# A fused retention and two-layer MLP kernel: the low part of the first eight weight tiles by a GpSimd subtraction instead of an adding DMA

## The chip, the cores and the metric

One NeuronCore of a Trainium2 chip runs the whole program. The metric is device time in microseconds (us), the median of several executions. Engines are named as in the profile: PE (TensorE), PEld (its weight loads), DVE (VectorE), ACT (ScalarE), POOL (GpSimd), SP (SyncE, which only issues DMAs here).

## What is computed

A retention layer (2 batches, 8 heads, 768 positions, head size 64) gives 1536 rows of 512 numbers; two MLPs follow, each 512 to 2048 to 512.

```python
for t in range(S):                                   # retention, y is [B, H, S, D]
    state = gamma * state + outer(k[:, :, t], v[:, :, t])
    y[:, :, t] = scale * einsum('bhd,bhde->bhe', q[:, :, t], state)
x = y.transpose(0, 2, 1, 3).reshape(1536, 512)
h = x @ w1_in;  x = softplus(h) @ w1_out             # maximum(h,0) + log1p(exp(-|h|))
h = x @ w2_in;  out = (h * clip(h + 3, 0, 6) / 6) @ w2_out
```

The four weight matrices come as 8-byte floats; the kernel gets them as pairs of 32-bit words.

## The kernel before

**Precision.** PE multiplies in a format with fewer mantissa bits than float32 (F32R). So every operand of the MLPs is kept as two tiles: a high part (the value rounded to F32R) and a low part (value minus high part). A product takes three matmuls: high by high, high by low, low by high.

**Weights.** The four matrices make 64 weight tiles of 128 x 512. `fetch` (L73) loads one as 512 KB of raw words on SP's queue. `convert` (L83) turns it into float32 in `w` and then into `w_parts`, high part in `t[:, 0]`, low part in `t[:, 1]`: ACT scales `raw`; DVE clamps it, shifts it, and merges it with two operations on two SBUF tiles each (L90 to L93, two TENSOR_SCALAR and two SCALAR_TENSOR_TENSOR in the profile); ACT writes minus the rounded value into `t[:, 1]` (L95); a DMA on POOL's queue adds `w` to it in place (L96); ACT writes the rounded value into `t[:, 0]` (L97). A buffer of `w` is free again when its adding DMA has landed.

**Order.** The list at L104 to L107 fixes which tile is converted when: four tiles of the first matrix (EARLY = 4), then tiles of the second and the first in turn, so that tiles number 4 and 6 (counted from 0) belong to the second matrix; then the second MLP's 32 tiles. `done[1]` counts converted tiles.

**Loops.** Four units of 128 rows of the retention run alone (L296). Then eight more units run in turn with the first eight of 96 steps (L144); after that the steps run alone. A step multiplies one 128-wide slice of the hidden layer for 512 rows (`gemm1`, 12 matmuls of 128 x 512, needs one tile of the first matrix), runs the activation over ACT and DVE, splits the result into `hi` (ACT) and `lo` (POOL for the first 16 steps, DVE later), and multiplies the slice of two steps before into the output banks (`gemm2`, 12 matmuls, needs one tile of the second matrix). The first 16 steps need tiles 0 to 31, two a step. A retention unit puts its score mask `pt`, its output `on` and the state update `bd` on DVE, and the decayed `vs`, the low part `x_lo` and the fading of `bd` on POOL.

A scheduler orders each engine's instructions after the first section (`nc.on = False` at L303) by its own estimate of times, so an edit in one place can move instructions elsewhere. A helper records nearly every instruction under L31, so tiles are told apart by name, not by line.

Of the kernel before, what the change touches and what calls it, by code (L numbers as in the profile page):

```python
# [10 lines left out]
F32 = mybir.dt.float32  # L11
F32R = mybir.dt.float32r
U32 = mybir.dt.uint32
AF = mybir.ActivationFunctionType
ALU = mybir.AluOpType
# [25 lines left out]
@with_exitstack  # L41
def kernel(ctx, tc, q, k, v, w1_in, w1_out, w2_in, w2_out, tq, tk, tc_, tg, out):
    nc = InOrder(tc)
    B, H, S, D = q.shape
    NT, DM = out.shape
    DFF = w1_in.shape[1]
    NP = H // 2
    KD = DM // P
    NF = DFF // P
    C = P  # L50
    NCH = S // C
    CH = 512
    chunks1 = [(0, 0, 512), (1, 0, 512), (2, 0, 512)]
    chunks2 = [(0, 0, 512), (1, 0, 512), (2, 0, 512)]
    LAG = 2
    EARLY = 4

    tc.nc.scalar.preload_act_table_set("softplus")

    xpool = ctx.enter_context(tc.tile_pool(name="xpool", bufs=1))  # L60
    x_hi = [xpool.tile([P, KD, CH], F32R, name=f"x_hi{c}") for c in range(NT // CH)]
    x_lo = [xpool.tile([P, KD, CH], F32R, name=f"x_lo{c}") for c in range(NT // CH)]

    win_p = ctx.enter_context(tc.tile_pool(name="win", bufs=NF))
    wout_p = ctx.enter_context(tc.tile_pool(name="wout", bufs=NF))
    psum = ctx.enter_context(tc.tile_pool(name="psum", bufs=1, space=PSUM))
    raw_p = ctx.enter_context(tc.tile_pool(name="raw", bufs=3))
    cv_p = ctx.enter_context(tc.tile_pool(name="cv", bufs=2))

    w_in_t, w_out_t, raws = {}, {}, {}  # L70
    words = {0: (w1_in.bitcast(U32), w1_out.bitcast(U32)), 1: (w2_in.bitcast(U32), w2_out.bitcast(U32))}

    def fetch(m, o, f):  # L73
        raw = raw_p.tile([P, CH, 2], U32, tag="raw", name="raw")
        src = words[m][o]
        if o:
            nc.sync.dma_start(out=raw.rearrange("p n t -> p (n t)"), in_=src[f * P:(f + 1) * P, :])
        else:
            nc.sync.dma_start(out=raw.rearrange("p (k n) t -> p k (n t)", k=KD),
                              in_=src[:, 2 * f * P:2 * (f + 1) * P].rearrange("(k p) f -> p k f", p=P))  # L80
        raws[m, o, f] = raw

    def convert(m, o, f):  # L83

        raw = raws.pop((m, o, f))
        low, y = raw[:, :, 0], raw[:, :, 1]

        w = cv_p.tile([P, CH], U32, tag="w", name="w")
        nc.scalar.activation(y.bitcast(F32), y.bitcast(F32), AF.Copy, scale=2.0 ** -112)
        nc.vector.tensor_scalar(y.bitcast(F32), y.bitcast(F32), -TOP, TOP, ALU.max, ALU.min)  # L90
        nc.vector.tensor_scalar(w, y, 3, None, ALU.logical_shift_left)
        nc.vector.scalar_tensor_tensor(w, y, 0x80000000, w, ALU.bitwise_and, ALU.bitwise_or)
        nc.vector.scalar_tensor_tensor(w, low, 29, w, ALU.logical_shift_right, ALU.bitwise_or)  # L93
        t = (wout_p if o else win_p).tile([P, 2, CH], F32R, tag="w", name="w_parts")
        nc.scalar.activation(t[:, 1], w.bitcast(F32), AF.Copy, scale=-1.0)  # L95
        nc.gpsimd.dma_start(out=t[:, 1].bitcast(F32), in_=w.bitcast(F32), accum_op=ALU.add)  # L96
        nc.scalar.activation(t[:, 0], w.bitcast(F32), AF.Copy)  # L97
        if o:
            w_out_t[m, f] = t
        else:  # L100
            w_in_t[m, f] = t.rearrange("p a (k n) -> p a k n", k=KD)

    NU = B * NCH
    order = [(0, 0, f) for f in range(EARLY)]  # L104
    for f in range(NF):
        order += [(0, 1, f)] + [(0, 0, f + EARLY)] * (f + EARLY < NF)
    order += [(1, 0, f) for f in range(NF)] + [(1, 1, f) for f in range(NF)]  # L107
    done = [0, 0]

    def fetch_weights(n):  # L110
        while done[0] < min(len(order), n):
            fetch(*order[done[0]])
            done[0] += 1

    def feed(n):

        n = min(n, len(order))
        while done[1] < n:
            fetch_weights(done[1] + (1 if nc.on else 2))
            convert(*order[done[1]])  # L120
            done[1] += 1

    banks = psum.tile([P, 8, CH], F32, name="banks")
    free = list(range(8))

    def bank(hold=False):

        i = free.pop(0)
        if not hold:
            free.append(i)  # L130
            return banks[:, i, :]
        return i, banks[:, i, :]

    def release(i):
        free.append(i)

    def first(f):
        return EARLY + 2 * (f + 1) - max(0, f + 1 + EARLY - NF)

    step, last, n_steps = moe(ctx, tc, nc, out, x_hi, x_lo, w_in_t, w_out_t, chunks1, chunks2, NF, KD, DM, CH, LAG, feed, first, bank, release)  # L140
    s = 0
    with ExitStack() as actx:
        unit = attention(actx, tc, nc, q, k, v, tq, tk, tc_, tg, x_hi, x_lo, CH, bank, feed, fetch_weights)
        for u in range(CH // P, NU):  # L144
            unit(u)
            step(s)
            s += 1
    while s < n_steps:
        step(s)
        s += 1  # L150
# [298 lines left out]
```

## Time and profile before

| what | value |
|---|---|
| median of 3 runs | 633.73 us (632.96 to 635.1) |
| the profiled execution | 632.11 us, its span 630.3 us |
| PE busy over the span | 600.6 us (95%) |
| DVE busy | 352.4 us (56%) |
| ACT busy | 281.1 us (45%) |
| POOL busy | 116.5 us (18%) |
| adding DMAs `w_parts<-w` | 64, 256 KB each |

The span is what the trace covers; 1.8 us lie around it. Shares are means over stages that are limited by different engines: the retention alone (to about 29 us), the stage in which weights are converted for the first 16 steps (about 29 to 187 us), and the rest, in which PE runs without gaps. Matmul ends are modelled, so a busy PE is not PE at its peak.

### The profile page before, as it was taken

The numbers are of one execution on the slowest core, as the hardware profiler recorded it, in microseconds if no ns is written. First come the engines' busy times: TensorE is split into PE (matmuls) and PEld (weight loads), VectorE is DVE, ScalarE is ACT, GpSimd is POOL, SyncE is SP. The second block draws the span as 40 slices with busy tenths as digits, with TensorE's granted clock in tenths as the row PEclk, the third lists the DMA queues.
The fourth block names the chain that finished last, engine by engine and source line by source line (L and its number), as shares of the span: only waits on it lengthen the run. The fifth ranks groups of instructions, "written<-read, shape, count | busy, mean of one in ns | idle before, by whom it ended". The sixth has DMA issues, their size and how long they took to land.

```text
span 630.3 us, 7793 instructions
## 1 busy us (share of the span) xinstructions
PE 600.6 (95%) x2963; PEld 493.1 (78%) x2963; DVE 352.4 (56%) x567; ACT 281.1 (45%) x481; POOL 116.5 (18%) x126
## 2 busy tenths in 40 slices
PE   7957979799989999999999999999999999999997
PEld 6846767678768888888887878888888888888886
DVE  4569988898856333357576789932232222422223
ACT  3327556667655333356556677832222222222221
POOL 1735655444420000011111122300000000000000
PEclk9979979799999999999999999999999999999999
DMA  9988986798750000025558688810010000100001
GB/s 193 227 230 222 255 212 152 185 214 203 168 131 1 0 1 0 1 43 125 113 138 216 151 203 218 198 33 1 0 68 0 1 0 2 68 0 1 0 1 67
DMA packets 70662, 63.70 MB, mean 101 GB/s; under 512 B 40160, under 2 KB 56800, under 8 KB 70624
## 3 DMA queue, kind: packets, MB, share of 16 engines
q1 hardware_dynamic: 61408, 46.42, 25.5%
q0 software_dynamic: 9216, 16.78, 16.1%
q8 instruction: 23, 0.38, 0.3%
q14 instruction: 15, 0.12, 0.1%
HBM read 43.26 MB, written 3.15 MB: 74 GB/s over the span
## 4 chain that ended last, share of the span: by engine, by line
PE 60%; DVE 10%; issue 6%; DMA 4%; ACT 4%; POOL 1%; DVEq 0%; POOLq 0%; ACTq 0%
PE banks L31 60%; DVE w L31 5%; DMA raw<-in_moe_w_in_dram 3%; DVE raw L31 2%; ACT w_parts L31 1%; DVE g L31 1%; ACT e L31 1%; DMA w_parts<-w 1%; DVE e L31 1%; ACT raw L31 1%; ACT hi L31 1%; POOL lo L31 1%; DVE lo L31 1%; DVE pt L31 0%; POOL w_parts L31 0%
## 5 line engine op out<-in xcount | busy, mean ns | idle before, releaser
L31 PE MATMUL banks<-x_hi,w_parts 128*128 128x512 f32 x768 | 255.2, 393 | 5.5 <-DMA w_parts<-w 5.5
L31 PEld LDWEIGHTS banks<-x_hi,w_parts 128*128 128x128 f32 x768 | 145.0, 189 | 36.4 <-DMA w_parts<-w 5.7
L31 PE MATMUL banks<-x_lo,w_parts 128*128 128x512 f32 x384 | 150.2, 391 | 0.0
L31 PE MATMUL banks<-hi,w_parts 128*128 128x512 f32 x384 | 127.0, 392 | 0.7 <-ACT hi L31 0.4
L31 PE MATMUL banks<-w_parts,hi 128*128 128x512 f32 (+1 forms) x386 | 118.5, 388 | 0.5 <-DVE g L31 0.5
L31 DVE SCALAR_TENSOR_TENSOR w<-raw,w 128x512 uint32<-128x512 uint32 x128 | 102.6, 801 | 2.0
L31 DVE SCALAR_TENSOR_TENSOR g<-e,banks 128x512 f32<-128x512 f32 x48 | 33.0, 688 | 125.2 <-ACT e L31 125.2
L31 POOL DMA_DIRECT2D w_parts<-w x64 | 55.9, 874 | 238.8 <-ACT w_parts L31 181.8
L31 ACT ACTIVATE w_parts<-w 128x512 fp32r<-128x512 f32 x128 | 74.3, 624 | 39.4 <-DVE w L31 38.7
L31 ACT ACTIVATE e<-banks,three 128x512 f32<-128x512 f32 x48 | 32.9, 686 | 127.6 <-PE banks L31 127.6
L31 ACT ACTIVATE hi<-g 128x512 fp32r<-128x512 f32 x96 | 60.6, 631 | 59.9 <-DVE g L31 59.1
L31 PEld LDWEIGHTS banks<-hi,w_parts 128*128 128x128 f32 x384 | 71.9, 188 | 17.1 <-ACT hi L31 1.6
L31 PEld LDWEIGHTS banks<-w_parts,hi 128*128 128x128 f32 x386 | 72.3, 188 | 15.8 <-DVE g L31 0.9
L31 PEld LDWEIGHTS banks<-x_lo,w_parts 128*128 128x128 f32 x384 | 72.7, 189 | 15.0 <-issue 0.3
L31 DVE TENSOR_TENSOR lo<-g,hi 128x512 fp32r<-128x512 f32 x80 | 55.3, 691 | 47.2 <-ACT hi L31 47.2
L31 PE MATMUL banks<-lo,w_parts 128*128 128x512 f32 x192 | 75.5, 393 | 2.3 <-POOL lo L31 2.1
L31 PE MATMUL banks<-w_parts,lo 128*128 128x512 f32 (+1 forms) x193 | 74.9, 388 | 0.0
L31 DVE SCALAR_TENSOR_TENSOR e<-g,banks 128x512 f32<-128x512 f32 x48 | 32.8, 683 | 33.0 <-ACT g L31 32.8
L31 ACT ACTIVATE raw<-raw 128x512 f32<-128x512 f32 x64 | 42.6, 668 | 17.0 <-DMA raw<-in_moe_w_in_dram 17.0
L31 DVE TENSOR_TENSOR g<-g,e 128x512 f32<-128x512 f32 x48 | 33.2, 691 | 27.4 <-ACT e L31 27.3
L31 PEld LDWEIGHTS banks<-lo,w_parts 128*128 128x128 f32 x192 | 36.0, 188 | 11.7 <-POOL lo L31 3.6
L31 ACT ACTIVATE g<-banks 128x512 f32<-128x512 f32 x48 | 28.3, 589 | 37.1 <-PE banks L31 36.7
(45 smaller groups left out, 413.8 us busy)
## 6 DMA issues: line engine op xcount, KB each, us to landing
raw<-in_moe_w_in_dram SPq DMA_DIRECT2D x32, 512.0 KB, 4.2
w_parts<-w POOLq DMA_DIRECT2D x64, 256.0 KB, 4.8
raw<-in_moe_w_out_dram SPq DMA_DIRECT2D x32, 512.0 KB, 4.5
q<-in_q_dram SPq DMA_DIRECT2D x12, 256.0 KB, 5.6
v<-in_v_dram SPq DMA_DIRECT2D x12, 256.0 KB, 4.9
k<-in_k_dram SPq DMA_DIRECT2D x11, 256.0 KB, 5.2
out_dram<-ob SPq DMA_DIRECT2D x11, 256.0 KB, 2.0
k<-in_k_dram SPq DMA_DIRECT2D x2, 128.0 KB, 2.7
```

The source lines that it names most:

```text
L31: ins = getattr(self.engine, op)(*args, **kwargs)
```

## The change

For the tiles converted while `done[1] < 8`, ACT writes the high part first, and POOL subtracts it from `w` into `t[:, 1]`; the negated copy and the adding DMA are gone for these eight tiles. The other 56 tiles are made as before.

```diff
         t = (wout_p if o else win_p).tile([P, 2, CH], F32R, tag="w", name="w_parts")
-        nc.scalar.activation(t[:, 1], w.bitcast(F32), AF.Copy, scale=-1.0)
-        nc.gpsimd.dma_start(out=t[:, 1].bitcast(F32), in_=w.bitcast(F32), accum_op=ALU.add)
-        nc.scalar.activation(t[:, 0], w.bitcast(F32), AF.Copy)
+        if done[1] < 2 * EARLY:
+            nc.scalar.activation(t[:, 0], w.bitcast(F32), AF.Copy)
+            nc.gpsimd.tensor_tensor(t[:, 1], w.bitcast(F32), t[:, 0].bitcast(F32), ALU.subtract)
+        else:
+            nc.scalar.activation(t[:, 1], w.bitcast(F32), AF.Copy, scale=-1.0)
+            nc.gpsimd.dma_start(out=t[:, 1].bitcast(F32), in_=w.bitcast(F32), accum_op=ALU.add)
+            nc.scalar.activation(t[:, 0], w.bitcast(F32), AF.Copy)
```

The scheduler's order moves with it. On PE, just after the last state update of the section that runs alone (`vs,k`), stood in the kernel before, with what each row waits for (DMASW is an adding DMA's semaphore):

```order
L31 MATMUL banks<-vs,k 128x128 x4
L31 MATMUL banks<-qT,kT 128x128 [waits Activation_49]
L31 MATMUL banks<-x_hi_59,w_parts 128x512 [waits Activation_49]
L31 MATMUL banks<-x_lo_62,w_parts 128x512 [waits Pool_49]
L31 MATMUL banks<-qT,kT 128x128 x7
L31 MATMUL banks<-x_hi_59,w_parts 128x512 [waits DMASW0_49]
L31 MATMUL banks<-x_hi_59,w_parts 128x512
```

In the changed kernel the same place reads:

```order
L31 MATMUL banks<-vs,k 128x128 x4
L31 MATMUL banks<-x_hi_59,w_parts 128x512 [waits Activation_49]
L31 MATMUL banks<-x_lo_62,w_parts 128x512 [waits Pool_49]
L31 MATMUL banks<-x_hi_59,w_parts 128x512 [waits Pool_49]
L31 MATMUL banks<-x_hi_59,w_parts 128x512
L31 MATMUL banks<-x_lo_62,w_parts 128x512
```

The first matmul that needs the low part of tile 0 waits for POOL and no longer for a DMA, and the scores `qT,kT` of the next unit stand behind the whole first `gemm1`.

On POOL, from the fade of `bd` in the fifth unit on, stood before:

```order
L31 TENSOR_TENSOR bd_112<-bd_112,tc_sb 64x4x64 [waits DVE_49,Pool_49]
L31 DMA w_parts<-w 128x512 [waits Activation_49]
L31 TENSOR_TENSOR vs<-v,tk_sb 128x512 [waits DMAHW3_49,Pool_49]
L31 TENSOR_TENSOR x_lo_63<-on,x_hi_60 128x4x128 [waits Activation_49]
L31 DMA w_parts<-w 128x512 [waits Activation_49] x2
L31 TENSOR_TENSOR lo<-g,hi 128x512 [waits Activation_49]
L31 TENSOR_TENSOR x_lo_63<-on,x_hi_60 128x4x128 [waits Activation_49]
```

In the changed kernel:

```order
L31 TENSOR_TENSOR bd_112<-bd_112,tc_sb 64x4x64 [waits DVE_49,Pool_49]
L31 TENSOR_TENSOR w_parts<-w,w_parts 128x512 [waits Activation_49,Pool_49]
L31 TENSOR_TENSOR x_lo_63<-on,x_hi_60 128x4x128 [waits Activation_49]
L31 TENSOR_TENSOR vs<-v,tk_sb 128x512 [waits DMAHW3_49]
L31 TENSOR_TENSOR w_parts<-w,w_parts 128x512 [waits Activation_49]
L31 TENSOR_TENSOR vs<-v,tk_sb 128x512 [waits DMAHW6_49]
L31 TENSOR_TENSOR lo<-g,hi 128x512 [waits Activation_49]
L31 TENSOR_TENSOR w_parts<-w,w_parts 128x512 [waits Activation_49]
L31 TENSOR_TENSOR x_lo_63<-on,x_hi_60 128x4x128 [waits Activation_49]
```

Each subtraction is one more reader and writer of SBUF among those that POOL had.

On DVE, around the shift into `w` of tile 11 (the shifts are the rows `w<-raw`), stood before, with the wait for the adding DMA of tile 8 (number 0 of its semaphores for the second time):

```order
L31 SCALAR_TENSOR_TENSOR w<-raw,w 128x512 [waits DVE_49]
L31 TENSOR_SCALAR raw<-raw 128x512 [waits DMAHW7_49,Activation_49]
L31 TENSOR_SCALAR w<-raw 128x512 [waits DMASW0_49,DVE_49]
L31 SCALAR_TENSOR_TENSOR w<-raw,w 128x512 [waits DVE_49]
L31 TENSOR_TENSOR on<-banks,tq_sb 128x512 [waits PE_49,Pool_49]
```

In the changed kernel tile 11's shift has no such wait, and the one for the DMA of tile 8 (there the first of all) comes at tile 12:

```order
L31 TENSOR_SCALAR raw<-raw 128x512 [waits DMAHW6_49,Activation_49]
L31 TENSOR_SCALAR w<-raw 128x512 [waits DVE_49]
L31 SCALAR_TENSOR_TENSOR w<-raw,w 128x512 [waits DVE_49]
L31 TENSOR_SCALAR raw<-raw 128x512 [waits DMAHW0_49,Activation_49]
L31 TENSOR_TENSOR on<-banks,tq_sb 128x512 [waits PE_49,Pool_49]
L31 TENSOR_SCALAR w<-raw 128x512 [waits DMASW0_49,DVE_49]
```

The ring of `w` buffers is one deeper by these waits.

## Rows read from the trace of the kernel before

**Rows 1.** The page's busy times by engine, and its chain that ended last.

```profile
PE 600.6 (95%) x2963; PEld 493.1 (78%) x2963; DVE 352.4 (56%) x567; ACT 281.1 (45%) x481; POOL 116.5 (18%) x126
PE 60%; DVE 10%; issue 6%; DMA 4%; ACT 4%; POOL 1%; DVEq 0%; POOLq 0%; ACTq 0%
```

**Rows 2.** Busy time by stretch: length, engines (instructions), granted PE clock, DMA share, GB/s.

```profile
40.00:60.00 20.00, 13.85 (x90) 11.35 (x91) 14.29 (x20) 10.68 (x20) 6.17 (x6) 0.84 0.94 245
60.00:80.00 20.00, 19.72 (x129) 14.73 (x130) 19.71 (x29) 11.37 (x21) 13.95 (x12) 1.00 1.00 240
120.00:160.00 40.00, 40.00 (x199) 32.63 (x199) 36.37 (x60) 27.00 (x48) 18.35 (x17) 0.98 0.81 194
29.04:192.00 162.96, 140.98 (x800) 112.24 (x799) 134.96 (x209) 96.31 (x173) 76.12 (x74) 0.94 0.80 193
```

**Rows 3.** The chain around 186 us: start, length, what.

```profile
185.31 1.28 POOL lo L31
186.63 108.92 PE banks L31 x479
```

**Rows 4.** Timeline of tile 0 (start, length, engine, operation, [idle before]), and its DMA's landing.

```profile
33.63 1.15 ACT L31 ACTIVATE w_parts<-w 128x512 fp32r<-128x512 f32 x2 [2.68 <-DVE w L31]
34.60 1.02 POOL L31 DMA_DIRECT2D w_parts<-w  x1 [1.73 <-ACT w_parts L31]
42.90 1.22 PE L31 MATMUL banks<-x_hi,w_parts 128*128 128x512 f32 x2 [5.51 <-DMA w_parts<-w]
DMA to landing us min/median/max: 8.3/8.3/8.3
```

**Rows 5.** Timeline of DVE where it stood idle for adding DMAs or their followers.

```profile
43.36 0.43 DVE L31 TENSOR_SCALAR w<-raw 128x512 uint32<-128x512 uint32 x1 [1.95 <-DMA w_parts<-w]
43.82 0.69 DVE L31 SCALAR_TENSOR_TENSOR w<-raw,w 128x512 uint32<-128x512 uint32 x1
47.79 0.69 DVE L31 SCALAR_TENSOR_TENSOR e<-g,banks 128x512 f32<-128x512 f32 x1 [3.28 <-ACT g L31]
48.86 0.43 DVE L31 TENSOR_SCALAR raw<-raw 128x512 f32<-128x512 f32 x1 [0.38 <-ACT raw L31]
88.16 0.43 DVE L31 TENSOR_SCALAR w<-raw 128x512 uint32<-128x512 uint32 x1 [1.26 <-DMA w_parts<-w]
180.41 0.43 DVE L31 TENSOR_SCALAR w<-raw 128x512 uint32<-128x512 uint32 x1 [2.68 <-DMA w_parts<-w]
```

**Rows 6.** Timeline of PE: its last gap of the conversion stage.

```profile
186.63 0.50 PE L31 MATMUL banks<-lo,w_parts 128*128 128x512 f32 x1 [0.85 <-POOL lo L31]
```

**Rows 7.** Groups over the whole span: busy us, mean ns of one, idle before.

```profile
L31 DVE SCALAR_TENSOR_TENSOR w<-raw,w 128x512 uint32<-128x512 uint32 x128 | 102.6, 801 | 2.0
L31 DVE TENSOR_SCALAR raw<-raw 128x512 f32<-128x512 f32 x64 | 32.5, 510 | 5.5 <-ACT raw L31 5.2
L31 DVE TENSOR_SCALAR w<-raw 128x512 uint32<-128x512 uint32 x64 | 32.0, 500 | 11.4 <-DMA w_parts<-w 11.1
L31 POOL DMA_DIRECT2D w_parts<-w x64 | 55.9, 874 | 238.8 <-ACT w_parts L31 181.8 <-DVE w L31 56.8
L31 POOL TENSOR_TENSOR lo<-g,hi 128x512 fp32r<-128x512 f32 x16 | 22.3, 1395 | 26.6 <-ACT hi L31 26.6
```

**Rows 8.** Timeline of DVE and POOL where their work met, or did not.

```profile
51.46 5.07 DVE L31 SCALAR_TENSOR_TENSOR w<-raw,w 128x512 uint32<-128x512 uint32 x2
51.56 1.46 POOL L31 TENSOR_TENSOR lo<-g,hi 128x512 fp32r<-128x512 f32 x1
54.05 1.20 POOL L31 TENSOR_TENSOR vs<-v,tk_sb 128x512 f32<-128x512 f32 x1
84.42 1.47 POOL L31 TENSOR_TENSOR lo<-g,hi 128x512 fp32r<-128x512 f32 x1
84.68 1.28 DVE L31 TENSOR_TENSOR pt<-banks,tm_sb 128x512 f32<-128x512 f32 x2
```

**Rows 9.** Timeline of PE after a long wait for `pt`, and after a short one.

```profile
85.42 2.07 PE L31 MATMUL banks<-qT,bd 128*128 128x128 f32 x8 [3.18 <-DVE pt L31]
99.85 1.16 PE L31 MATMUL banks<-qT,bd 128*128 128x128 f32 x8 [1.27 <-DVE pt L31]
```

## The prediction

> **What bounds the kernel now.** I read the busy times and the chain that ended last first [rows 1]. PE is busy for 95% of the span, but a share of 10% of the chain lies on DVE, so some stage is not PE's. The chain in order of time says which: the last thing before an unbroken run on PE is a POOL subtraction that ends at 186.6 us, and from 186.63 us on 479 matmuls follow each other [rows 3]. All that comes later is PE's own and this change doesn't touch it. So the time moves by what the conversion stage, 29 to 187 us, moves.
>
> The table by stretch shows who is full there. DVE was busy 134.96 of 162.96 us between 29 and 192 us, 19.71 of 20 us from 60 to 80 us and 36.37 of 40 us from 120 to 160 us; PE was full too in those two stretches, but had 13.85 of 20 us from 40 to 60 us [rows 2]. ACT, with 96.31 of 162.96 us, and POOL, with 76.12, had room. The reader should see that DVE and PE take turns at being late, and that DVE, which has to convert 32 tiles in this stage, sets the pace for most of it: PE's last gap, at 186.63 us, is for a `lo` whose input came late from DVE [rows 6].
>
> **What the change removes.** Tile 0 shows the old price. ACT had its two copies done from 33.63 us on, POOL took 1.02 us to issue the adding DMA at 34.60 us, and the data landed 8.3 us after the issue; PE stood 5.51 us until 42.90 us [rows 4]. POOL's subtraction of the same shape and types exists already: `lo<-g,hi` takes 1.395 us on average [rows 7]. POOL ended its former work before ACT's copy did (it stood 1.73 us ahead of the DMA [rows 4]), so the low part of tile 0 should be there at about 33.6 + 0.6 (half of ACT's 1.15 for two) + 1.4 = 35.6 us instead of 42.9. PE's order has the whole first `gemm1` at that place, so its wait all but goes.
>
> PE's 5.5 us are not the gain, because DVE, not PE, is late after 49 us. What counts is the time that DVE stood still because of this DMA: 1.95 us for a buffer of `w` and 3.28 us for the first activation, which PE made late [rows 5]. **Term one: minus 5.2 us.** The 0.38 us behind it [rows 5] I leave out: ACT's order there moves too.
>
> The second place is the ring of `w` buffers. Tile 11 waited 1.26 us for the adding DMA of tile 8, and a late tile waited 2.68 us [rows 5]. With the ring one deeper by the order's waits, I count the first in full. The second only matters as far as PE waited behind it, 0.85 us [rows 6]. **Term two: minus 2.1 us.** It lies between 0, if the scheduler's new order has DVE wait elsewhere, and 3.9, the two waits together.
>
> ACT loses no copy that matters: it has one copy less in each of eight tiles, 0.6 us each, on an engine with room, so I cost that at nothing; its cover is ACT's idle time, 163 less 96 us. The 8 DMA issues that leave POOL give 8 x 0.874 = 7.0 us back [rows 7], the subtractions take 8 x 1.395 = 11.2. That 4.2 us more lies in POOL's idle time, 163 less 76 us, and costs nothing by itself. Behind a subtraction on POOL stand `vs`, `x_lo` and `lo`; each is late by at most the difference of 0.5 us a tile, which PE's backlog of matmuls covers from 60 us on [rows 2].
>
> **What the change adds: POOL beside DVE.** DVE's operations on SBUF tiles stand still while POOL works on SBUF. At 51.46 us two merges, 0.69 us each when undisturbed [rows 5], took 5.07 us, and ended 1.3 us after the last of three POOL operations between 51.56 and 55.25 us [rows 8]. That is 3.7 us lost to 3.7 us of POOL. But at 84.42 us a POOL subtraction ran its 1.47 us, while DVE, which read PSUM for `pt`, kept its 1.28 us for two [rows 8]: nothing lost. So the price of a subtraction is between 0 and its own length.
>
> The mean comes from the groups. Merges averaged 801 ns against 690 undisturbed, over 128 of them 14.2 us; the clamps 510 against 430, over 64, 5.1 us; the shifts 500 against 430, 4.5 us: 23.8 us in all [rows 5, 7]. POOL's work other than DMA issues in the stage was 76.12 less 32 x 0.874 = 48.2 us [rows 2, 7]. So DVE lost 0.49 us for each us of POOL. Eight subtractions of 1.395 us are 11.2 us, and **term three is plus 5.5 us**, between 0 and 11.2. I take the mean, since the eight are spread over the same mixture of DVE's work. The order bears this out in part: behind tile 1's shift stand `e` and both `pt`, which read PSUM, but tiles 2, 3 and 6 meet merges and shifts.
>
> On this the Trainium skill, SBUF — State Buffer, section Who interferes with whom, says that the two engines share one port pair as an exclusive lock, and that an instruction with two SBUF inputs, or in a two-port mode, waits for the whole of the other's instruction. The merges at 51.46 us agree. Taken alone the rule would make term three 11.2 us; the sum above doesn't use it.
>
> **Sum.** -5.2 - 2.1 + 5.5 = -1.8 us. Against the profiled execution that is 632.1 - 1.8 = 630.3 us; its time stands 1.6 us under the median of the runs, and the forecast is for a median, so 633.7 - 1.8 = **631.9 us**. A measurement of this kernel can tell about 0.3%, 1.9 us, from no change, so this lies on the border.
>
> **Rival 1: the locks fall on covered work.** If the eight subtractions meet DVE mostly while it reads PSUM, as at 84.42 us, term three is 0 and the gain is 7.3 us: 626.4 us. For it speaks tile 1's place. Against it speaks the mean, and that DVE's conversions are the larger part of its work here.
>
> **Rival 2: each subtraction locks DVE for its whole length.** The place is DVE between 34 and 75 us, where the eight subtractions are. Then term three is 11.2 us, and the sum +3.9 us: 637.6 us, slower. It decides from 7.3 / 8 = 0.91 us of lost DVE time a subtraction, 65% of its length. For it speaks 51.46 us, where POOL operations back to back kept DVE out entirely, and that the new order sets subtractions next to `x_lo`, `vs` and `lo`. A late `pt` would add to it: after 3.18 us of waiting for `pt`, PE's next eight small matmuls took 2.07 us, at the half of its two clock levels, against 1.16 after a wait of 1.27 us [rows 9]. The page named above is the rule behind this rival. Against it speaks that the mean loss is 49%.
>
> **Rival 3: the early tiles buy nothing.** PE is ahead at 40 us, and DVE waits as long elsewhere, for `pt`'s inputs or for raw tiles, because the conversion order is the same. Then the first two terms and the third cancel, 633.7 us. For it speaks that DVE's work is unchanged in number; against it that the two waits of 1.95 and 3.28 us have no other cause than the DMA.
>
> **How the numbers follow.** Forecast 0.40, with term three between 35% and 65% of 11.2 us, so 630.3 to 633.7 us; half of that is faster by over 0.3%. Rival 1 has 0.23, rival 2 0.24, rival 3 0.13. Faster: 0.20 + 0.23 = 0.43. Within 0.3%: 0.18 from the forecast and 0.11 from rival 3, 0.29. Slower: 0.24 of rival 2 and 0.04 of what the scheduler's new order may cost in the other two, 0.28. The range reaches from rival 1 to rival 2: 626.0 to 637.7 us. The forecast's own range is 630.3 to 633.7 us.
>
> **What would show it.** In the changed profile, PE's wait of 5.5 us at 42.9 us should be gone and the first `gemm1` be over by about 39 us. DVE's two idle pieces of 1.95 and 3.28 us should be gone. Merges, clamps and shifts should take some 5.5 us more in all than 102.6 + 32.5 + 32.0 us: near 0 proves rival 1, near 11 rival 2. The unbroken run on PE should begin near 185 us instead of 186.6, and be as long as before. I am wrong if PE has new gaps after 60 us for `pt` or tiles, with its clock at the half level behind them, or if the stage after 187 us changes.

## The result and the profile after

The changed kernel took 624.85 us in the median (623.2 to 626.26, 4 runs), the kernel before 633.35 us beside it (631.57 to 635.1, 4 runs). The ratio is 0.9874, with a 95% interval of 0.984 to 0.9908: 1.26% or 8.0 us faster. (Here and below the ratio compares runs taken side by side and is not exactly the quotient of the two medians, which would be 0.9866.) The forecast was 631.9 us with a range of 626.0 to 637.7, so the time fell 1.15 us below the range. The profiled execution of the changed kernel is 623.2 us, its span 621.4 us, 8.9 us less than the 630.3 of before.

The page's busy times by engine, and its chain that ended last, answer to [rows 1]:

```profile
PE 597.2 (96%) x2963; PEld 491.9 (79%) x2963; DVE 355.6 (57%) x567; ACT 277.9 (45%) x473; POOL 122.3 (20%) x126
PE 67%; DVE 9%; issue 4%; ACT 3%; POOL 1%; DMA 1%; DVEq 0%; ACTq 0%; POOLq 0%
```

The busy time by stretch answers to [rows 2] (length, engines with instructions, granted PE clock, DMA share, GB/s):

```profile
40.00:60.00 20.00, 17.66 (x117) 13.91 (x114) 19.91 (x27) 10.48 (x20) 11.84 (x9) 0.86 0.84 218
60.00:80.00 20.00, 16.32 (x105) 12.63 (x104) 19.77 (x27) 10.57 (x19) 13.22 (x11) 0.89 0.75 189
120.00:160.00 40.00, 39.58 (x190) 32.32 (x187) 36.09 (x60) 29.28 (x52) 19.08 (x18) 1.00 0.83 198
29.04:192.00 162.96, 145.41 (x834) 117.31 (x833) 144.60 (x218) 98.90 (x175) 82.81 (x74) 0.96 0.74 180
```

DVE now is full from 40 to 80 us, 19.91 and 19.77 of 20 us, where it had 14.29 from 40 to 60 us [rows 2]. The timeline of tile 0 answers to [rows 4]; of POOL, and of PE:

```profile
33.96 1.28 POOL L31 TENSOR_TENSOR w_parts<-w,w_parts 128x512 fp32r<-128x512 f32 x1 [0.33 <-ACT w_parts L31]
```

```profile
35.26 0.77 PE L31 MATMUL banks<-x_hi,w_parts 128*128 128x512 f32 x1
...
38.76 0.39 PE L31 MATMUL banks<-x_hi,w_parts 128*128 128x512 f32 x1
```

The first `gemm1` runs from 35.26 to 39.1 us without a gap. The end of the stage, on DVE (the late wait of [rows 5]) and on PE [rows 6]:

```profile
171.50 0.43 DVE L31 TENSOR_SCALAR w<-raw 128x512 uint32<-128x512 uint32 x1 [2.43 <-DMA w_parts<-w]
```

```profile
177.72 0.50 PE L31 MATMUL banks<-lo,w_parts 128*128 128x512 f32 x1 [0.79 <-POOL lo L31]
```

PE's last gap ends at 177.72 us where it ended at 186.63. That is 8.9 us, all of the difference between the spans, so all of the gain arose in the conversion stage. The groups over the span answer to [rows 7] (busy us, mean ns, idle before):

```profile
L31 DVE SCALAR_TENSOR_TENSOR w<-raw,w 128x512 uint32<-128x512 uint32 x128 | 102.0, 797 | 1.9
L31 DVE TENSOR_SCALAR raw<-raw 128x512 f32<-128x512 f32 x64 | 35.1, 548 | 5.5 <-ACT raw L31 5.3
L31 DVE TENSOR_TENSOR g<-g,e 128x512 f32<-128x512 f32 x48 | 34.4, 716 | 27.2 <-ACT e L31 27.2
L31 DVE TENSOR_SCALAR w<-raw 128x512 uint32<-128x512 uint32 x64 | 32.7, 511 | 8.1 <-DMA w_parts<-w 7.7
```

Merges, clamps and shifts took 169.8 us after 167.1, and `g<-g,e`, which reads two SBUF tiles as well, 34.4 after 33.2. Its row in the kernel before:

```profile
L31 DVE TENSOR_TENSOR g<-g,e 128x512 f32<-128x512 f32 x48 | 33.2, 691 | 27.4 <-ACT e L31 27.3
```

In all, DVE lost 3.9 us more, where 5.5 was forecast. With that the sum would be -5.2 - 2.1 + 3.9 = -3.4 us, and -8.0 was measured. What made up the rest is what the experiments are for.

### The profile page after: what moved, and what is told of

Read it like the earlier page. It is cut to its first block, busy times and chain, and to the rows that moved or that the text cites. A ratio compares the mean times of both kernels' runs of the same rounds, so it can differ in the third digit from the quotient of the medians.

```text
span 621.4 us, 7753 instructions
## 1 busy us (share of the span) xinstructions
PE 597.2 (96%) x2963; PEld 491.9 (79%) x2963; DVE 355.6 (57%) x567; ACT 277.9 (45%) x473; POOL 122.3 (20%) x126
## 4 chain that ended last, share of the span: by engine, by line
PE 67%; DVE 9%; issue 4%; ACT 3%; POOL 1%; DMA 1%; DVEq 0%; ACTq 0%; POOLq 0%
PE banks L31 67%; DVE w L31 5%; DVE raw L31 1%; ACT w_parts L31 1%; DVE g L31 1%; DMA raw<-in_moe_w_in_dram 1%; ACT e L31 1%; DVE e L31 1%; DVE lo L31 1%; ACT hi L31 1%; POOL lo L31 0%; POOL bd L31 0%; DVE pt L31 0%; POOL w_parts L31 0%; DVE bd L31 0%
## 5 line engine op out<-in xcount | busy, mean ns | idle before, releaser
L31 DVE SCALAR_TENSOR_TENSOR w<-raw,w 128x512 uint32<-128x512 uint32 x128 | 102.0, 797 | 1.9
L31 POOL DMA_DIRECT2D w_parts<-w x56 | 49.0, 876 | 220.4 <-ACT w_parts L31 163.5
L31 ACT ACTIVATE w_parts<-w 128x512 fp32r<-128x512 f32 x120 | 69.9, 624 | 42.3 <-DVE w L31 37.7
L31 DVE TENSOR_TENSOR g<-g,e 128x512 f32<-128x512 f32 x48 | 34.4, 716 | 27.2 <-ACT e L31 27.2
```

Source lines behind the costliest of these rows:

```text
L31: ins = getattr(self.engine, op)(*args, **kwargs)
```

## Experiments: parts of the change, and its two prices

Ratios below are to the kernel before, measured beside each run, with 95% intervals; 0.01 is 6.3 us.

**Tile 0 alone, and tiles 1 to 7 alone.**

```diff
-        if done[1] < 2 * EARLY:
+        if done[1] < 1:
```

> Only tile 0 gets its low part by the GpSimd subtraction, tiles 1 to 63 by the adding DMA. Start-up theory (the 8.3 us landing of tile 0's DMA is nearly the whole cost, and the lead is kept because TensorE and VectorE then stop waiting for each other): 6 to 9 us faster than before, 625 to 627.5 us. Theory that every early tile's landing counts: one eighth to a third of the gain, 1 to 3 us, 630.5 to 632.5 us. Theory that the scheduler's new order is what helps: any time between 624 and 634 us, with no tie to the wait of 5.5 us.

Measured: 626.99 us, ratio 0.9896 (0.9854 to 0.9939), -6.6 us.

```diff
-        if done[1] < 2 * EARLY:
+        if 1 <= done[1] < 8:
```

> Tile 0 by the adding DMA as before, tiles 1 to 7 by the GpSimd subtraction. Start-up theory: the 5.5 us wait of TensorE is still there, so at most 2 us faster than before, 631.5 to 634 us. Theory that every early tile counts: 5 to 8 us faster, 625.5 to 628.5 us. Scheduler theory: anything between 624 and 636 us.

Measured: 630.13 us, ratio 0.9952 (0.9933 to 0.9972), -3.0 us. Tile 0 has the larger part of the gain, as term one had it. Each of the two runs has an order of its own, though, so this is not the work alone. The order of the run with tile 0 alone differs from that of the kernel before in one short stretch only, between 34 and 57 us: some 20 of PE's 2963 matmuls, 30 of DVE's 567 rows and 14 of ACT's and POOL's, and two loads just ahead of it. One subtraction and this stretch make 6.6 us.

**The gain without the lock, and the lock without the gain.** In the first run ScalarE makes the low part as a scaled copy, so that neither a DMA nor POOL is needed (the values differ); in the second POOL's eight subtractions are added to the kernel before.

```diff
-            nc.gpsimd.tensor_tensor(t[:, 1], w.bitcast(F32), t[:, 0].bitcast(F32), ALU.subtract)
+            nc.scalar.activation(t[:, 1], w.bitcast(F32), AF.Copy, scale=2.0 ** -13)
```

> For the first eight tiles the low part is written by one ScalarE copy (a scaled copy of w, so the low part is not the remainder), with neither the GpSimd subtraction nor the adding DMA: the cover without VectorE's lock. If the eight subtractions cost what the two traces say (VectorE busy 3.2 us more between the same two points): 3 us faster than the changed kernel, 621 to 623 us. If they cost nothing on the way to the end: as the changed kernel, 624 to 626 us. If they cost their length (11.2 us): 614 us.

Measured: 619.14 us, ratio 0.9776 (0.974 to 0.9812), -14.2 us.

```diff
         nc.scalar.activation(t[:, 0], w.bitcast(F32), AF.Copy)
+        if done[1] < 2 * EARLY:
+            nc.gpsimd.tensor_tensor(spare, w.bitcast(F32), t[:, 0].bitcast(F32), ALU.subtract)
```

> The kernel before, with one more GpSimd subtraction of the same shape into a spare tile for each of the first eight tiles, nothing removed: the lock without the cover. Mean lock price of the record (0.49 us of VectorE a us of GpSimd): plus 5.5 us, 638 to 640 us. Price by the two traces: plus 3 us, 636 to 637 us. Whole-length lock: plus 11, 644 us. Covered work: within 1 us of before.

Measured: 639.85 us, ratio 1.0109 (1.0077 to 1.0141), +6.9 us. Read together these said: the lock costs some 6 to 7 us, a little over term three, and its removal uncovers 14 us where terms one and two had 7.3. So the gain looked twice too small.

**Where the 14 us are: buffers held, traffic, or issue.** To the run with ScalarE's copy an adding DMA into a spare tile was added, which nobody waits for: reading `w` (its buffer is held until it lands), reading `w_parts` (it is not held), and reading 4 columns of `w` only. In all three POOL also zeroes the spare tiles, from 1.6 to 5.4 us, ahead of the other work.

```diff
+            nc.gpsimd.dma_start(out=SPARE[done[1]], in_=w.bitcast(F32), accum_op=ALU.add)
```

> As e3 (low part of the first eight tiles by a ScalarE copy, not the remainder), plus for each of the eight an adding DMA of the same size from w into a spare tile that nobody reads: traffic, issue and the hold on the w buffer are back, only TensorE's wait for the landing is gone. If the 14 us that e3 gained lie in TensorE's waits for landings: still 12 to 14 us under before, 618 to 621 us. If they lie in the w ring that the landings hold: back to within 4 us of before, 629 to 633 us.

Measured: 623.13 us, ratio 0.9868 (0.9834 to 0.9902).

```diff
+            nc.gpsimd.dma_start(out=SPARE[done[1]], in_=t[:, 1].bitcast(F32), accum_op=ALU.add)
```

> As e5, but the spare adding DMA reads the finished low part and not w, so the w buffers come free early: only the traffic and the issue are back. If the traffic of eight adding DMAs is what costs: close to before, 629 to 633 us. If not: as e3, 618 to 621 us. The difference to e5 is the price of the hold on w.

Measured: 623.82 us, ratio 0.9873 (0.9849 to 0.9896). The two are the same, so holding the buffers costs nothing that can be seen, though here ScalarE's later copies waited 7.1 us for these DMAs. (The orders of the two differ, in some 160 of DVE's rows.) Both lose some 6 us against the run without DMAs, which I first put down to the traffic of 8 x 256 KB. The third run tests this:

```diff
+            nc.gpsimd.dma_start(out=SPARE[done[1]][:, :4], in_=w[:, :4].bitcast(F32), accum_op=ALU.add)
```

> As the run in which ScalarE makes the low part of the first eight tiles by a scaled copy (so these low parts hold other values, and no subtraction runs), and in which an adding DMA of the tile was kept; here that kept DMA takes only 4 of the 512 columns: POOL still issues eight DMAs (0.87 us each in the trace of before), but 2 KB in place of 256 KB moves. If the eight DMAs cost their 6 us by what they move (ScalarE alone 619.1 us against 623.1 with the DMAs), this run gives about 619 us, with raw tiles landing in some 4 to 5 us as without them. If the cost is in their issue on POOL, or in the other order that the scheduler makes around eight more DMAs, it stays at about 623 us.

Measured: 624.31 us, ratio 0.9888 (0.9862 to 0.9915). With 2 KB in place of 256 KB a DMA the loss stays, 7.1 us against the run without DMAs. This run has nearly the order of the first of the three (PE's and ACT's rows are the same, nine of DVE's stand elsewhere), so the two differ by what the DMAs move and by little else. The theory of the traffic falls; left are the issue on POOL, and the order that the scheduler makes around eight more instructions.

**How many tiles.** The same change for four and for sixteen tiles:

```diff
-        if done[1] < 2 * EARLY:
+        if done[1] < 4:
```

> The change for the first four tiles alone. Tile 0 alone gave -6.6 us, the eight -8.2. If each further tile saves some traffic (0.75 us a tile) and pays a lock (0.8 us a tile), the curve is flat and this gives about 626 us, -7. If tiles 4 to 7 are the ones that gain nothing and only lock DVE, it is better than the eight: 622 to 623 us. If the gain comes from the ring of buffers of w, whose wait at tile 11 only the whole eight removes, it stays near tile 0 alone, 627 us.

Measured: 619.31 us, ratio 0.9813 (0.9786 to 0.984), -11.8 us: faster than both kernels.

```diff
-        if done[1] < 2 * EARLY:
+        if done[1] < 16:
```

> The change for the first sixteen tiles. If traffic saved and lock paid cancel for each further tile, about 624 us, as with eight. If locks cost more where DVE is full (60 to 130 us), eight more of them at 0.8 us a tile without cover give some 630 us. If the transfers are still what the later tiles wait for, another 3 us less, 621 us.

Measured: 631.57 us, ratio 1.0001 (0.9981 to 1.002): nothing gained. From one tile to four, eight and sixteen the gain goes 6.6, 11.8, 8.0, 0.0 us. A fixed price and a fixed gain for each tile would not give this curve.

**DVE in place of POOL.**

```diff
-            nc.gpsimd.tensor_tensor(t[:, 1], w.bitcast(F32), t[:, 0].bitcast(F32), ALU.subtract)
+            nc.vector.tensor_tensor(t[:, 1], w.bitcast(F32), t[:, 0].bitcast(F32), ALU.subtract)
```

> The low part of the first eight tiles by a subtraction on DVE instead of POOL: the adding DMAs are gone as in the change, and what is paid is DVE's own time, eight times about 0.7 us (a merge of the same shape takes 0.69 us undisturbed), with no lock. If the end moves by DVE's time one for one, the run with ScalarE (619.1 us) plus 5.6 gives 624.7 us, the same as the change. If the lock costs more than DVE's own work would (0.8 us a tile from the runs, and 1.39 us of POOL each), this is faster than the change, 622 to 624 us. If the order on DVE with eight more instructions is what counts, it is slower, above 627 us.

Measured: 623.97 us, ratio 0.9884 (0.9859 to 0.9908), the same as the change. DVE's group of the eight subtractions in this run:

```profile
L31 DVE TENSOR_TENSOR w_parts<-w,w_parts 128x512 fp32r<-128x512 f32 x8 | 6.5, 818 | 0.0
```

Eight subtractions on POOL cost the end about as much as 6.5 us of DVE's own work, each in an order of its own: some 190 of DVE's 567 rows and 350 of PE's matmuls stand elsewhere, so this does not part price from order.

**Without the scheduler.** `nc.on = True` in place of `False` keeps the whole program in the order in which it is written, before and after the change. The same switch lets `feed` fetch only one raw tile ahead in place of two, so the distance from the kernels above is not the order's alone; the two runs have it alike.

> The kernel before with every engine's instructions kept in the order of the program text to the end, so the scheduler moves nothing. A base for e8 only; I expect it slower than before, 640 to 670 us.

Measured: 769.9 us, ratio 1.2187 (1.2162 to 1.2213).

> The changed kernel in the same fixed order as e7: the same cover and lock, with the scheduler out. If the gain of the change comes from cover and not from the scheduler's new order: 5 to 11 us under e7. If the order made it: within 2 us of e7.

Measured: 771.34 us, ratio 1.2221 (1.2173 to 1.227). There the change gains nothing. The first `gemm1` starts at 40.89 and 40.66 us in the two and waits for no landing, since it stands late in the program anyway. So the gain is not there in every order; that it needs one in which tile 0 is urgent fits this, but is not shown. It doesn't tell work from order in the kernel as it is.

## Experiments: one kernel's work in another's order

To part work from order, six kernels keep the work of one kernel and chain every engine's instructions, by edges that carry no wait, in the order that the scheduler had made for another. Where the two differ, the DMA stands in the subtraction's place and the other way round. In the traces each engine's rows stand in the other kernel's order, one by one. By their own orders the kernel before and the changed one differ in some 170 of DVE's 567 rows and 220 of PE's 2963 matmuls.

```diff
     while s < n_steps:
         step(s)
         s += 1
+    keep_order(tc)
```

> The work of the kernel before (64 adding DMAs), with every engine's instructions in the order that the scheduler gave the changed kernel; the adding DMA stands where the subtraction stands, and the negated copy directly ahead of the high part's. If the 8 us come from the work that is removed, this is no faster than before, some 632 us, or slower by up to 8 us, since in this order PE has the first gemm1 whole at the place where it waits for tile 0's landing. If the new order brings the gain, about 625 us.

Measured: 628.29 us, ratio 0.9962 (0.9943 to 0.998), -2.4 us.

> The work of the changed kernel (eight subtractions on POOL) with every engine's instructions in the order of the kernel before. If the gain is in the work, 624 to 626 us. If it is in the order, 632 us, and more by what the locks cost there (up to 7 us).

Measured: 628.23 us, ratio 0.996 (0.9942 to 0.9979), -2.5 us.

> The run in which ScalarE makes the low part of the first eight tiles by a scaled copy (their values differ), in the order of the run that had eight DMAs of four columns besides, and without these DMAs. If issuing a DMA on POOL costs DVE or POOL 5 us in eight, this gives 619 us, as in the order of its own. If only the order made the run with the small DMAs slower, it gives 624 us.

Measured: 624.52 us, ratio 0.9897 (0.9875 to 0.9918).

> The kernel before in the order of the run that had eight subtractions more on POOL (639.9 us), without these. If the 7 us more were the lock's, it gives 632 us, as the kernel before. If they were the order's, 639 us. In between, the difference from 639.9 is the price of eight subtractions at an order held fast.

Measured: 630.27 us, ratio 0.9981 (0.9959 to 1.0002). This order turns out to be nearly that of the kernel before: no row of PE, DVE or ACT stands elsewhere, on POOL two neighbours have changed places, on SP a few loads. So the run also says what the chaining itself does, which is nothing clear of noise.

> The change for the first four tiles, in the order that the change for eight has. If what tiles 4 to 7 cost (624.9 against 619.3 us) is the work of four subtractions on POOL, this gives 619 to 621 us. If it is the order, about 625 us.

Measured: 623.1 us, ratio 0.9866 (0.984 to 0.9891).

> The change for all eight tiles, in the order that the change for four has. If tiles 4 to 7 cost 5.5 us by their work (four subtractions with their locks), this gives 624 to 625 us. If by their order, 619 us.

Measured: 625.18 us, ratio 0.9894 (0.9874 to 0.9914).

All in one table, rows are work, and the ratio stands under the order that it ran in:

| work | its own order | another's order |
|---|---|---|
| before | 1 | 0.9962 (of after), 0.9981 (of before with eight subtractions more) |
| the change | 0.9874 | 0.996 (of before), 0.9894 (of first four) |
| first four tiles | 0.9813 | 0.9866 (of after) |
| ScalarE's low part | 0.9776 | 0.9897 (of the run with eight 4-column DMAs) |
| before and eight subtractions more | 1.0109 | |

- **The change's work alone, in the old order, gives -2.5 us** (0.996). The new order alone, with the old work, gives -2.4 us (0.9962). Together they give -8.0, so some 3 us belong to neither alone: the new order is worth more when the landing is gone, and the work is worth more in the new order. By either way of counting the order gives 2.4 to 5.4 us and the work 2.5 to 5.6.
- **Eight issues on POOL cost nothing that can be told.** ScalarE's copy in the order of the run with the small DMAs is 0.9897, with these DMAs 0.9888. The 7 to 8 us between 0.9776 and them are the order's.
- **Eight subtractions cost up to 8 us at an order held fast:** 1.0109 less 0.9981 is 0.0128, 8.1 us, give or take 2.4. But tiles 4 to 7 cost nothing that can be told in the order of after (0.9874 against 0.9866) and 5 us in the order of the four (0.9894 against 0.9813). So the price is one of the place.

**What the old order does with the gain.** The three fences show PE where it waits for `pt` behind the second `gemm1`: in the kernel before, in the changed work in the old order (L85 is the same helper in a longer file), and in the changed kernel.

```profile
54.81 0.39 PE L31 MATMUL banks<-vs,k 128*128 128x128 f32 x2
58.45 0.43 PE L31 MATMUL banks<-pt,vs 128*64 128x128 f32 x2 [3.25 <-DVE pt L31]
```

```profile
47.76 0.39 PE L85 MATMUL banks<-vs,k 128*128 128x128 f32 x2
54.19 0.69 PE L85 MATMUL banks<-pt,vs 128*64 128x128 f32 x2 [6.05 <-DVE pt L85]
...
56.11 0.77 PE L85 MATMUL banks<-x_hi,w_parts 128*128 128x512 f32 x1
```

```profile
48.08 1.06 PE L31 MATMUL banks<-vs,k 128*128 128x128 f32 x8
48.89 0.47 PE L31 MATMUL banks<-x_hi,w_parts 128*128 128x512 f32 x1
...
52.67 0.43 PE L31 MATMUL banks<-pt,vs 128*64 128x128 f32 x2 [1.92 <-DVE pt L31]
...
56.86 0.80 PE L31 MATMUL banks<-hi,w_parts 128*128 128x512 f32 x1
```

In the old order PE comes to this place 7.05 us earlier (47.76 after 54.81), but `pt` only 4.26 us earlier (54.19 after 58.45). PE's wait grows from 3.25 to 6.05 us, with the third `gemm1` behind it. In the new order PE has seven of that `gemm1`'s twelve matmuls ahead of the wait, which is 1.92 us, and at 56.86 us it is in the first `gemm2`, while the old order begins the third `gemm1` at 56.11. The two later waits for `pt` in the old order, and the two longest in the new:

```profile
84.36 2.08 PE L85 MATMUL banks<-qT,bd 128*128 128x128 f32 x8 [3.24 <-DVE pt L85]
112.30 2.08 PE L85 MATMUL banks<-qT,bd 128*128 128x128 f32 x8 [3.66 <-DVE pt L85]
```

```profile
96.94 1.16 PE L31 MATMUL banks<-qT,bd 128*128 128x128 f32 x8 [3.55 <-DVE pt L31]
110.56 1.16 PE L31 MATMUL banks<-qT,bd 128*128 128x128 f32 x8 [2.75 <-DVE pt L31]
```

In the old order PE's clock is at the half level behind both (2.08 us for eight, as at 85.42 us in [rows 9]), in the new one at the full level.

Since the rows of the kernel before and of the changed work in the old order are the same but for the eight, they can be compared one by one. The shifts into `w` start at (us):

| shift of tile | before | the change in the old order | lead |
|---|---|---|---|
| 4 | 57.38 | 52.65 | 4.7 |
| 7 | 71.89 | 70.30 | 1.6 |
| 10 | 83.61 | 82.56 | 1.1 |
| 20 | 130.71 | 127.42 | 3.3 |
| 33 | 180.41 | 177.07 | 3.3 |

DVE has nearly the whole of term one at tile 4, and has lost all but 1.1 us of it at tile 10. In between lie the subtractions of tiles 4 to 7, from 58.36 to 75.36 us. Some of it comes back later.

**The old work in the new order.** PE, and then DVE:

```profile
41.64 1.22 PE L85 MATMUL banks<-x_hi,w_parts 128*128 128x512 f32 x2 [6.30 <-DMA w_parts<-w]
```

```profile
46.95 0.69 DVE L85 SCALAR_TENSOR_TENSOR e<-g,banks 128x512 f32<-128x512 f32 x1 [6.86 <-ACT g L85]
```

Here DVE stands 6.86 us in one piece behind the landing of tile 0, where before it stood 1.95 and 3.28 us [rows 5], and still this kernel is 2.4 us faster than before. What the new order gives later is more than this loss.

**PE's clock in the four.** The same 2963 matmuls kept PE busy for 600.6 us before [rows 1] and for 597.2 in the changed kernel. The pages of the changed work in the old order and of the old work in the new order, whose spans are 628.2 and 626.7 us, have:

```profile
PE 601.4 (96%) x2963; PEld 494.2 (79%) x2963; DVE 355.1 (57%) x567; ACT 277.2 (44%) x473; POOL 122.4 (19%) x126
```

```profile
PE 599.0 (96%) x2963; PEld 491.3 (78%) x2963; DVE 350.0 (56%) x567; ACT 281.9 (45%) x481; POOL 117.9 (19%) x126
```

With the new work, the new order shortens the span of the profiled executions by 6.8 us, from 628.2 to 621.4. Of these, 4.2 us are time in which PE was busy with the same matmuls, and 2.6 us are its idle time. The granted clock of all runs, in the mean, goes the same way:

| work | order | runs | granted clock |
|---|---|---|---|
| before | before | 25 | 0.983 |
| the change | before | 10 | 0.984 |
| before | after | 10 | 0.987 |
| the change | after | 4 | 0.991 |

So more than half of what the new order gives the new work shows as less time at the half of PE's two clock levels. Whether the clock is a cause of its own here, or follows from where PE's waits lie, no run parts; and it is not all, for the run with the subtraction on DVE has the highest clock of all, 0.9955, and 623.97 us.

**The lock at one order.** The groups of DVE in the kernel before in the order of the run with eight subtractions more, and in that run itself:

```profile
L85 DVE SCALAR_TENSOR_TENSOR w<-raw,w 128x512 uint32<-128x512 uint32 x128 | 100.2, 783 | 2.0
L85 DVE TENSOR_SCALAR raw<-raw 128x512 f32<-128x512 f32 x64 | 33.3, 522 | 6.8 <-ACT raw L85 6.5
L85 DVE TENSOR_TENSOR g<-g,e 128x512 f32<-128x512 f32 x48 | 33.2, 691 | 27.4 <-ACT e L85 27.3
L85 DVE TENSOR_SCALAR w<-raw 128x512 uint32<-128x512 uint32 x64 | 32.9, 513 | 7.6 <-DMA w_parts<-w 7.2
```

```profile
L31 DVE SCALAR_TENSOR_TENSOR w<-raw,w 128x512 uint32<-128x512 uint32 x128 | 108.5, 848 | 2.0
L31 DVE TENSOR_TENSOR g<-g,e 128x512 f32<-128x512 f32 x48 | 35.8, 746 | 27.8 <-ACT e L31 27.7
L31 DVE TENSOR_SCALAR w<-raw 128x512 uint32<-128x512 uint32 x64 | 34.4, 537 | 10.2 <-DMA w_parts<-w 9.8
L31 DVE TENSOR_SCALAR raw<-raw 128x512 f32<-128x512 f32 x64 | 31.7, 496 | 5.5 <-ACT raw L31 5.2
```

The four groups are 199.6 and 210.4 us: DVE lost 10.8 us to eight subtractions of 11.8 us, and the end moved by 8.1. The same four groups with and without the change's work, in each of the two orders (us):

| group | before | the change, old order | before, new order | the change |
|---|---|---|---|---|
| merges `w<-raw,w` | 102.6 | 97.6 | 100.2 | 102.0 |
| clamps `raw<-raw` | 32.5 | 32.5 | 30.2 | 35.1 |
| shifts `w<-raw` | 32.0 | 38.2 | 34.0 | 32.7 |
| `g<-g,e` | 33.2 | 34.2 | 33.7 | 34.4 |
| sum | 200.3 | 202.5 | 198.1 | 204.2 |

In the old order DVE loses 2.2 us to 11.1 us of POOL, in the new order 6.1. The 2.2 us are a balance: the shifts lose 6.2 us, and the merges win 5.0 (two that took 5.07 us at 51.46 us before [rows 8] take 3.31 us at 47.64). How a subtraction holds DVE in one place and not in another is seen in the old order, on DVE and on POOL:

```profile
41.58 1.39 DVE L85 TENSOR_SCALAR w<-raw 128x512 uint32<-128x512 uint32 x1
...
47.64 3.31 DVE L85 SCALAR_TENSOR_TENSOR w<-raw,w 128x512 uint32<-128x512 uint32 x2
...
52.05 0.67 DVE L85 SCALAR_TENSOR_TENSOR e<-g,banks 128x512 f32<-128x512 f32 x1
```

```profile
41.35 1.33 POOL L85 TENSOR_TENSOR w_parts<-w,w_parts 128x512 fp32r<-128x512 f32 x1 [3.07 <-ACT w_parts L85]
...
47.28 1.45 POOL L85 TENSOR_TENSOR lo<-g,hi 128x512 fp32r<-128x512 f32 x1
...
51.81 1.45 POOL L85 TENSOR_TENSOR w_parts<-w,w_parts 128x512 fp32r<-128x512 f32 x1
```

The subtraction at 41.35 us holds a shift (1.39 us where 0.43 is its time undisturbed [rows 5]); the one at 51.81 us meets `e<-g,banks`, which reads PSUM and keeps its 0.67 us. The Trainium skill, SBUF — State Buffer, section Who interferes with whom, says that the blocked one waits for the other's whole instruction; the traces agree where the two meet, as with 10.8 of 11.8 us, and show with 2.2 of 11.1 us that they need not meet.

## Why the prediction was wrong

- **What bounds the kernel** was right. The whole 8.9 us lie before PE's unbroken run, and the run begins at 177.72 us in place of 186.63, where 185 was forecast.
- **Term one (-5.2 us)**: the cause was right. PE's wait is gone, the first `gemm1` is over at 39.1 us (39 was forecast), and DVE's pieces of 1.95 and 3.28 us [rows 5] are gone in both orders. In the old order 4.7 us of it have reached DVE's shift of tile 4 and 4.26 us the place of `pt`, at 54.19 after 58.45 us. PE then stands 2.8 us longer, and at tile 10 DVE's lead is down to 1.1 us.
- **Term two (-2.1 us)** did not come in the old order. In the changed kernel the piece of 1.26 us at tile 11 is gone and the late one stays, 2.43 us after 2.68, for the landing of tile 31 in both kernels: the ring is deeper for the early tiles alone. The table of DVE's waits for adding DMAs (us in total, times, longest) has, before and with the new work in the old order:

```profile
DVE w L31 <- DMA w_parts<-w: 5.9, 3, 2.7
```

```profile
DVE w L85 <- DMA w_parts<-w: 3.8, 3, 2.2
```

They fell by 2.1 us, which looks like term two; but 1.95 us of the 5.9 are the piece that term one has counted [rows 5]. Without it 3.9 us became 3.8, and 2.4 in the changed kernel.

- **Term three (+5.5 us)** lay between what different orders show: 2.2, 6.1 and 10.8 us, at DVE. The mean of the trace was a fair value; a fixed 0.49 us of DVE for each us of POOL there is not. The sum of merges, clamps and shifts, named as the sign, rose by 2.7 us from the one kernel to the other, between rivals 1 and 2.
- **The sum, -1.8 us, is close to what the work does in the old order, -2.5 us** (0.9942 to 0.9979, so 1.3 to 3.7). That is luck in good part: at DVE term two was near 0 there in place of -2.1, and term three 2.2 in place of 5.5, two errors of opposite sign.
- **The step that failed** is "how the numbers follow", where the scheduler's new order stands as a cost of 0.04 on the side of slower, and nowhere as a gain: its gain was put at nothing, and no reason was given. The sum was made for instructions in their old places, but for the three places of the order that were shown. The runs show a gain in its place: with the old work the new order gave 2.4 us (0.9962), with the new work 5.4 us (from 0.996 to 0.9874, give or take 2.4 us), more than the sum itself. The range's lower end was rival 1's price, so it had no room for it.
- **Costs put at nothing**: the eight issues on POOL cost nothing that could be told (0.9888 with them, 0.9897 without), as costed. That POOL's additional time hides was not tried by itself.
- **The rivals.** Rival 1's 626.4 us came near the result by number, but its mechanism did not happen: in the order of after the locks took 6.1 us of DVE. Rival 2's mechanism is real in the run with subtractions alone, at 8.1 us. Rival 3 happens in part: in the old order DVE's later work takes most of PE's gain back through `pt`, and DVE's lead of 4.7 us shrinks to 1.1.
- **What would show it** named new gaps for `pt` behind 60 us as the sign of being wrong. There are such gaps, 2.07 us at 68 us, 3.55 and 2.75 us, without the half level behind the latter two. But they were no sign: the kernel before has its own, 3.18 us at 85.42 us [rows 9] and 4.32 us at 115.28 us, both with the half level behind them (2.07 and 2.08 us for eight matmuls). In all, PE waited for `pt` 12.7 us in five pieces before and 14.3 us in nine in the changed kernel, which was faster for all that.

What stays open: why just this order is better. The place at 48 to 57 us is shown, and the run with tile 0 alone, whose order is new from 34 to 57 us only, points to it with its 6.6 us; that it carries all of the 5.4 us is not shown. The time at the half level, 4.2 of the 6.8 us between the two profiled executions, is a second part that no run took by itself.

## What to carry to other kernels

Where a scheduler sets the order from its own estimates, an edit has two effects, the work and the new order, and the second was here as large as the first: in four of the six pairs of the table the order moved the same work by 0.4 to 1.2%; in the other two, of which one has nearly the same order, by 0.2%, which is not clear of noise. Cost the edit in the old order, then give the range at least the spread that orders make, on both sides, and part the two by running one's work in the other's order. And try several sizes: four tiles (619.31 us, 0.9813) were better than eight (624.85), and sixteen gained nothing, each in the order that the scheduler gave it.

## What the runs showed of the hardware

A subtraction on POOL reaches more of DVE's work than merges, clamps and shifts: `g<-g,e` went from 691 to 746 ns in the mean of 48 with eight subtractions. The length of a wait alone did not set PE's level afterwards: behind 3.55 us at 96.94 us eight small matmuls took 1.16 us, behind 3.24 us in the other order 2.08. And eight adding DMAs from SBUF to SBUF that no matmul waits for cost the end nothing that could be told, whether each moved 256 KB (0.9868, 0.9873) or 2 KB (0.9888; without them, in the same order, 0.9897).
